# Sums and remainders on 32 columns of TensorE once per pair of rows, and the column sums of the last stage after the fill, in a fused backward kernel

## The chip, the cores and the metric

One core of a Trainium2 chip runs the whole program in one launch. The metric is the device time in microseconds (us) of that launch. The core has a matmul engine (TensorE, PE in the profile, its weight loads shown as PEld), three engines for elementwise work (VectorE, DVE; ScalarE, ACT; GpSimd, POOL) and SyncE (SP), which here only issues DMA transfers. ScalarE and GpSimd issue transfers too. Each engine works through its own list of instructions in order, and engines wait for each other through semaphores.

## The reference

The reference is one block of a network with 2048 rows and 576 columns in bfloat16: a modulation vector from `silu(c) @ w_mod`; LayerNorm, modulation, a spectral filter (`rfft2`, times `w_r + i w_i`, `irfft2`) and a residual; LayerNorm, modulation, a gated product and a residual. Its forward part is

```
mod = (silu(c) @ w_mod).reshape(1, 6, 1, 576)      # sa, ca, ga, sb, cb, gb
h = layernorm(x) * (1 + ca) + sa
x = x + ga * irfft2(rfft2(h) * (w_r + 1j * w_i))
h = layernorm(x) * (1 + cb) + sb
x = x + gb * (((h @ w_gate) * (h @ w_up)) @ w_down)
```

The kernel returns the output (o0) and the gradients with respect to x, w_r, w_i, w_gate, w_up, w_down, c and w_mod. For the modulation vectors it needs sums over all 2048 rows of products that the two LayerNorm backwards form; the change moves matmuls that make such sums.

## The kernel before

The 2048 rows are held as 16 "rows" of 128 partitions by 576 columns (row j below is such a slab, not a matrix row). SBUF is one tile, `arena`, cut by hand into views and rings, and PSUM is one tile, `bank`, of eight banks, so nearly all names in the profile are `arena` and `bank`, and instructions are told apart by their line. The order of TensorE's instructions is the order in which the program writes them. The other engines' orders, and those of their DMA queues, are set by a planner from costs and due times, so moving matmuls on TensorE can move instructions on every other engine.

The stages, in order: gradient of the gated product's output, and the forward spectral filter; forward and backward of the gated product in 18 blocks (lines 796 to 990, some 900 us); LayerNorm 2 backward; backward of the spectral filter (lines 1324 to 1361); the last stage, which is its last transform and LayerNorm 1 backward; a short end for the gradients of c and w_mod.

A `Fill` (line 163) is a list of closures with costs. `fill.run(us)` emits as many as its credit covers. In LayerNorm 2 backward the fill holds the weight gradients of the last two blocks: `gwd_halves` (line 882 on PE, its products read out by VectorE in 889 and 890), `gw_block` (904 and 908, read out by ScalarE in 909) and `gw_rem` (924, on 64 columns, read out in 930). From the backward of the spectral filter on, it holds the forward's last product, o0, in pieces of nine matmuls (`y_piece`, line 1106; four pieces make one half of a row, which ScalarE copies out in 1109; two banks take turns; VectorE finishes a row in 1112 and 1113, and 1115 stores it).

LayerNorm 2 backward is the loop `for j in range(19)` (line 1180). TensorE ends the last block's product (`gh2_last`, 963 to 966, added up by VectorE in 985) three rows and more ahead; the n of a row is loaded by SP (1064) into the space that this frees. For even j, `front` (1130 to 1136) and `back` (1142 to 1150) do the elementwise work of a pair of rows on VectorE and ScalarE. SP also issues the saved rows y (1068), the stores of gx (1147), tables (1173), and the transposes of the weight gradients (850). Then, on TensorE:

- `sums_1(j)`: two `quarter_sums`, four matmuls (line 1047) of 32 columns each, one in each column quarter of the array, that add row j to sums over all rows in bank 2. It ran once per row, at j + 1.
- `sums_2(i)`: the same form, four matmuls into bank 5, once per pair.
- `row_a(j)`: four full-width matmuls (line 443) that begin the next transform of row j and, for odd j, the four remainders of the pair (446 and 447, 32 columns each), read out by ScalarE in 453 and 461. Banks come from a ring of six that the fill uses too.

The sums are read at the end of this stage by VectorE (1257 and 1258). W rows for the next stage are loaded on SP (515, 517) and by GpSimd as indirect loads (518); GpSimd also clears and sets a small table `sel` (1250 to 1255).

The last stage is the loop `for j in range(18)` (line 1395). `stage_bi(j)` makes four full-width matmuls (579, 581) and two on 32 rows of the array (582, 583); ScalarE copies one bank (585), VectorE combines it with the other (587, 588). `column_sums` (line 1041: four matmuls on 64 columns, into banks 6 and 7) added row j - 2 to its sums. `stage_ai(j - 1)` (593, two full-width matmuls) gives gh, copied by ScalarE (1409). The row's elementwise work follows: 1411, 1418, 1419 and 1421 on ScalarE, 1415 to 1423 on VectorE, the store 1425 on GpSimd. Then 36 matmuls of fill per row. VectorE has further work between: `mod_grad` (1278, 1279), on w_mod loaded by SP (1274), stored by GpSimd (1282). x and gx rows are loaded by SP in 1072 into rings of four: x of row j + 2 is asked for at row j, and its buffer is that of row j - 2, last read by 1421. The rings gh and q, which `column_sums` reads, have three buffers. Other loads of this stage on SP are 1087 (operands of the fill) and 1099 (x1). At the end the sums are copied (1439) to R2, which feeds the gradients of c and w_mod (1443 to 1477) and the last part of out_8 (1457, 1459, 1462).

Of the kernel before, what the change touches and what calls it, by code (L numbers as in the profile page):

```python
# [81 lines left out]
def build(ctx, tc, A_x, A_w_r, A_w_i, B_w_gate, B_w_up, B_w_down, c_in, w_mod, grad_out,  # L82
          out_0, out_1, out_2, out_3, out_4, out_5, out_6, out_7, out_8):
    nc = tc.nc
    pe, ve, ac, po, sp = nc.tensor, nc.vector, nc.scalar, nc.gpsimd, nc.sync
# [124 lines left out]
    with tc.manual_schedule(engines={PE}):  # L210
# [115 lines left out]
        def single():  # L326
            sbank[0] = (sbank[0] + 1) % 3
            return sbank[0]
# [112 lines left out]
        def stage_a(fj, b):  # L441
            for m in range(4):
                mm(bank[:, b, 128 * m:128 * m + 128], fj[:, FB[m]:FB[m] + 128], bdf, True, True)

        def stage_a_rem(fj, b, sub):
            mm(bank[0:32, b, 128 * sub:128 * sub + 128], fj[:, 256:288], bdf, True, True)
            mm(bank[32:64, b, 128 * sub:128 * sub + 128], fj[:, 544:576], bdf, True, True)

        def evac_a(eng, b, j):
            dst = At[:, 0:4, :, 8 * j:8 * j + 8]  # L450
            src = bank[:, b, :].rearrange("p (m c b) -> p m c b", m=4, c=16)
            if eng is ac:
                ac.copy(dst, src)
            else:
                ve.tensor_copy(dst, src)

        def evac_rem(eng, brem, j0, n):
            dst = At[0:64, 4, :, 8 * j0:8 * (j0 + n)].rearrange("p c (j b) -> p j c b", j=n)
            src = bank[0:64, brem, 0:128 * n].rearrange("p (j c b) -> p j c b", j=n, c=16)
            if eng is ac:  # L460
                ac.copy(dst, src)
            else:
                ve.tensor_copy(dst, src)
# [155 lines left out]
        for jg in range(4):  # L619
# [8 lines left out]
            for jj in range(4):  # L628
                b = single()
# [156 lines left out]
        def sbk():  # L786
            sbank[0] += 1
            return sring[sbank[0] % len(sring)]
# [167 lines left out]
        def acc_b(j):  # L956

            return acc[:, j, 0:288].bitcast(BF)
# [20 lines left out]
        def gh2_last(j):  # L979

            for h in range(2):
                b = sbk()
                gh2_mms(NP - 1, j, h, bank[:, b, 0:288])
                hs = slice(288 * h, 288 * h + 288)
                tt(acc_b(j)[:, hs], acc[:, j, hs], bank[:, b, 0:288], ADD)
# [51 lines left out]
        def column_sums(srcs, b, j, w):  # L1037

            for h in range(2):
                for i, a in enumerate(srcs):  # L1040
                    mm(bank[w * i:w * i + w, b + h, 0:288], ones[:, 0:w], a[:, 288 * h:288 * h + 288], j == 0, j == 15, skip_group_check=True)

        def quarter_sums(a, b, q, start, stop):

            for h in range(2):
                r = slice(32 * (q + h), 32 * (q + h) + 32)
                mm(bank[r, b, 0:288], ones[:, 0:32], a[:, 288 * h:288 * h + 288], start, stop, skip_group_check=True)
# [14 lines left out]
        def load_n(j):  # L1062
            if j < 14:
                sp.dma_start(acc_h(j), n_d[:, j, :])

        def load_yl(i):
            yl[i] = yl_r.next()
            sp.dma_start(yl[i][:], y_d[:, 2 * i:2 * i + 2, :])
# [53 lines left out]
        st_a = {}  # L1122
# [4 lines left out]
        def front(i):  # L1127
            gn, t2, q, s = gn_r.next(), t2_r.next(), q_r.next(), s_r.next().rearrange("p (k v) -> p k v", k=2)
            n, opc = n_pair(i), two(mod[:, SCB, :])
            tt(gn[:], b_pair(i), opc, MUL)  # L1130
            tt(q[:], b_pair(i), n, MUL)
            tt(t2[:], q[:], opc, MUL)
            for k in range(2):
                j = 2 * i + k
                act(gn[:, k, :], gn[:, k, :], ACT.Copy, scale=rstd2[:, j:j + 1], accum_out=s[:, k, 0:1])
                act(t2[:, k, :], t2[:, k, :], ACT.Copy, scale=nrs2[:, j:j + 1], accum_out=s[:, k, 1:2])
            st_a[i] = (gn, t2, q, s)
# [14 lines left out]
        def sums_1(j):  # L1152
            quarter_sums(acc_b(j), 2, 0, j == 0, j == 15)
            quarter_sums(st_a[j // 2][2][:, j % 2, :], 2, 2, j == 0, j == 15)
# [3 lines left out]
                quarter_sums(st_a[i][1][:, k, :], 5, 2 * k, i == 0, i == 7)  # L1158

        def row_a(j):  # L1160
            Fj = st_a[j // 2][0]
            b = sbk()
            stage_a(Fj[:, j % 2, :], b)
            evac_a(ac, b, j)
            if j % 2:
                b = sbk()
                for i in range(2):
                    stage_a_rem(Fj[:, i, :], b, i)
                evac_rem(ac, b, j - 1, 2)

        def load_third(t, name, k):
            n = 1536
# [7 lines left out]
        for j in range(19):  # L1180
            want = min(16, 3 + 5 * j // 4)
            while done < want:
                gh2_last(done)
                done += 1
                if done < want:
                    fill.run(1.0)
            while loaded < min(done, j + 6):
                load_n(loaded)
                loaded += 1
            if j % 2 == 0 and j < 16:  # L1190
                front(j // 2)
                back(j // 2)
                if 2 <= j < 14:
                    load_yl(j // 2 + 1)
            if fill.left() > 12.0 or j > 15:
                fill.run(1.0 if j < 16 else 2.0)
            if 1 <= j < 17:
                sums_1(j - 1)
            if fill.left() > 12.0 or j > 15:
                fill.run(1.0)  # L1200
            if 3 <= j:
                if j % 2 == 0:
                    sums_2(j // 2 - 2)
                row_a(j - 3)
            if j == 4:
                sp.dma_start(TB.rearrange("p a b -> p (a b)"), tabs["TB"][:, :])
            if 6 <= j < 9:
                load_third(TC, "TC", j - 6)
            if j == 12:
                for i0 in range(9, 28, 5):  # L1210
                    load_wdr(i0, min(28, i0 + 5))
                for k in range(3):
                    load_third(TI, "TI", k)
                sp.dma_start(TBI.rearrange("p a b -> p (a b)"), tabs["TBI"][:, :])
            if j == 15:
                for t in W_r.t:
                    po.memset(t[:, :, :, DF:FP], 0.0)
                for u in range(2):
                    Ws[u] = W_r.next()
                    load_W(Ws[u], u)  # L1220
            if j == 16:
                load_wdr(0, 6)
# [171 lines left out]
        mdone, gq = 0, {}  # L1394
        for j in range(18):
            if j < 16:
                if j and j + 2 < 16:
                    load_xg(j + 2)
                Hs[j] = stage_bi(j, Gt, e_r, H_r)
            if j > 1:  # L1400

                column_sums(gq.pop(j - 2), 6, j - 2, 64)
            if j < 2:
                store_rev(6 + j, gws[6 + j])
            if 1 <= j < 17:
                jj = j - 1
                stage_ai(Hs[jj])
                gh = gh_r.next()
                ac.copy(halves(gh), bank[:, 2:4, 0:288])
                n = xl[jj]  # L1410
                act(n[:], n[:], ACT.Identity, bias=nmr1[:, jj:jj + 1], scale=rstd1[:, jj:jj + 1])
                gn, t2, q, s = tg_r.next(), t2_r.next(), q_r.next(), s_r.next()
                gq[jj] = [gh, q]
                opc = mod[:, SCA, :]
                tt(gn[:], gh[:], opc, MUL)
                tt(q[:], gh[:], n[:], MUL)
                tt(t2[:], q[:], opc, MUL)
                act(gn[:], gn[:], ACT.Copy, scale=rstd1[:, jj:jj + 1], accum_out=s[:, 0:1])
                act(t2[:], t2[:], ACT.Copy, scale=nrs1[:, jj:jj + 1], accum_out=s[:, 1:2])
                ts(s[:, 0:1], s[:, 0:1], -1.0 / D, None, MUL)  # L1420
                act(t2[:], n[:], ACT.Identity, bias=s[:, 0:1], scale=s[:, 1:2])
                tt(gn[:], gn[:], t2[:], ADD)
                tt(gn[:], gn[:], gl[jj][:], ADD)
                o1 = gn
                po.dma_start(o1_v[:, jj, :], o1[:])
                fill.run(2.2)
            fill.run(2.2)
            while mdone < min(18, 6 * j // 5):
                k, i = mdone // 3, mdone % 3
                mod_grad(*mgs[k], i)  # L1430
                if i == 2 and k + 2 < 6:
                    load_wm2(mgs[k + 2][0], mgs[k + 2][2])
                mdone += 1
            if 5 <= j < 14:
                i = j - 5
                sp.dma_start_transpose(out=wmT[:, i, :], in_=w_mod[:, 128 * i:128 * i + 128])
# [100 lines left out]
```

## Time and profile before

| | us |
|---|---|
| runs shown (five) | 1488.18 to 1492.09, median 1489.47 |
| profiled execution | 1490.96 |
| its span, first to last instruction | 1489.2 |
| PE busy in the span | 1449.6 (97%) |
| VectorE, ScalarE, GpSimd busy | 766.5, 540.7, 347.3 |
| mean granted TensorE clock | 0.994 |
| LayerNorm 2 backward, first to last sum (line 1047) | 1187.6 to 1262.8 |
| last stage, first to last column sum (line 1041) | 1378.2 to 1476.3 |

Times within the profile are us from the first instruction. Matmuls are pipelined: one of 288 columns is shown 0.29 us long, but a stream of them has a start every 0.12 us, so a busy PE says only that something was in it. What one costs is read from the distance of starts. "<-" names what ended an engine's wait. The granted clock is the share of full speed that TensorE had. A line number can be that of a helper that many places call.

### The profile page before, as it was taken

To read this page: it belongs to the slowest core of one execution; us is meant where nothing else is said; L and a number is where in the kernel's file an instruction comes from. 1 tells how busy PE (TensorE), PEld (TensorE's weight loads), DVE (VectorE), ACT (ScalarE), POOL (GpSimd) and SP (SyncE) were. 2 spreads that over 40 slices of the span, in tenths; PEclk is the share of its full clock that TensorE was granted. 3 is DMA by queue.
4 is the path that set the end of the run, shared out by engine and by line. 5 is a ranking of instruction groups with operands and counts; after the bars stand their busy time and mean duration, and the time that the engine had idled before them with its cause. 6 is when DMAs were issued, how large, how long until landed. Compare 5 with 4: busy or idle time off the path is not lost.

```text
span 1489.2 us, 28224 instructions
## 1 busy us (share of the span) xinstructions
PE 1449.6 (97%) x11085; PEld 975.9 (66%) x11108; DVE 766.5 (51%) x1651; ACT 540.7 (36%) x1048; POOL 347.3 (23%) x510
## 2 busy tenths in 40 slices
PE   8999998999999999999999999999999998999988
PEld 5444444677677677677677677677677666677666
DVE  6533596533543543543543543543443687677655
ACT  6756675212222222222222222222212366334565
POOL 1344322213213203203203203203202013332211
PEclk9999999999999999999999999999999999999999
DMA  9656886968568559559549558558548289667863
GB/s 340 185 150 158 230 238 163 206 147 190 119 120 192 122 115 195 126 108 198 127 105 194 122 112 202 116 111 202 130 93 184 75 245 309 215 187 206 260 201 96
DMA packets 417050, 252.79 MB, mean 170 GB/s; under 512 B 319730, under 2 KB 384692, under 8 KB 416660
## 3 DMA queue, kind: packets, MB, share of 16 engines
q1 hardware_dynamic: 388706, 166.53, 49.4%
q0 software_dynamic: 27440, 83.65, 18.6%
q8 instruction: 87, 1.43, 0.4%
q10 hardware_dynamic: 770, 0.80, 0.2%
q14 instruction: 47, 0.39, 0.1%
HBM read 98.52 MB, written 76.26 MB: 117 GB/s over the span
## 4 chain that ended last, share of the span: by engine, by line
PE 81%; DVE 7%; DMA 5%; ACT 4%; issue 2%; SPq 0%; DVEq 0%; ACTq 0%
PE bank L808 8%; PE bank L857 8%; PE bank L810 8%; PE bank L904 8%; PE bank L908 8%; PE bank L1106 6%; PE bank L963 5%; PE bank L965 5%; PE bank L966 5%; PE bank L964 5%; PE bank L371 3%; PE bank L375 3%; PE bank L802 2%; PE bank L924 2%; DMA arena<-in_w_mod_dram 2%
## 5 line engine op out<-in xcount | busy, mean ns | idle before, releaser
L977 DVE TENSOR_TENSOR arena<-arena,bank 128x576 f32<-128x576 f32 x256 | 193.1, 754 | 305.1 <-PE bank L966 305.1
L816 ACT CAST arena<-bank 128x512 bf16<-128x512 f32 x144 | 86.6, 602 | 396.2 <-PE bank L803 387.7
L966 PE MATMUL bank<-arena 128*128 128x288 bf16 x576 | 164.5, 286 | 0.0
L963 PE MATMUL bank<-arena 128*128 128x288 bf16 x576 | 164.0, 285 | 0.4 <-DVE arena L975 0.2
L965 PE MATMUL bank<-arena 128*128 128x288 bf16 x576 | 164.3, 285 | 0.0
L964 PE MATMUL bank<-arena 128*128 128x288 bf16 x576 | 164.1, 285 | 0.0
L1106 PE MATMUL bank<-arena 128*128 128x288 bf16 x1152 | 152.4, 291 | 4.5 <-ACT arena L1109 4.5
L904 PE MATMUL bank<-arena 128*128 128x256 bf16 x1152 | 149.5, 273 | 1.8 <-DVE arena L890 1.8
L908 PE MATMUL bank<-arena 128*128 128x256 bf16 x1152 | 149.3, 273 | 0.0
L808 PE MATMUL bank<-arena 128*128 128x512 bf16 x576 | 148.2, 380 | 0.0
L810 PE MATMUL bank<-arena 128*128 128x512 bf16 x576 | 147.8, 379 | 0.0
L1106 PEld LDWEIGHTS <-arena 128*128 128x128 bf16 x1152 | 113.5, 100 | 38.1 <-issue 7.3
L857 PE MATMUL bank<-arena 128*128 128x288 bf16 x1024 | 128.1, 286 | 0.0
L820 DVE TENSOR_TENSOR arena<-arena 128x512 bf16<-128x512 bf16 x144 | 60.8, 422 | 123.4 <-ACT arena L816 116.3
L904 PEld LDWEIGHTS <-arena 128*128 128x128 bf16 x1152 | 110.8, 98 | 18.6 <-issue 5.2
L908 PEld LDWEIGHTS <-arena 128*128 128x128 bf16 x1152 | 112.3, 98 | 13.7
L857 PEld LDWEIGHTS <-arena 128*128 128x128 bf16 x1024 | 100.2, 98 | 28.2
L735 POOL DMA_DIRECT2D arena<-ghh_d x36 | 19.9, 553 | 392.9 <-DVE arena L819 385.1
L909 ACT CAST arena<-bank 128x256 bf16<-128x256 f32 x144 | 52.6, 372 | 141.8 <-PE bank L908 141.6
L810 PEld LDWEIGHTS <-arena 128*128 128x128 bf16 x576 | 56.4, 98 | 68.0
L808 PEld LDWEIGHTS <-arena 128*128 128x128 bf16 x576 | 53.4, 98 | 71.7 <-issue 15.5
L817 ACT CAST arena<-bank 128x512 bf16<-128x512 f32 x144 | 85.7, 595 | 12.2 <-PE bank L810 11.6
(269 smaller groups left out, 2303.4 us busy)
## 6 DMA issues: line engine op xcount, KB each, us to landing
ghh_d<-arena POOLq DMA_DIRECT2D x72, 256.0 KB, 3.6
arena<-ghh_d POOLq DMA_DIRECT2D x36, 512.0 KB, 6.2
hh_d<-arena SPq DMA_DIRECT2D x36, 512.0 KB
arena<-hh_d SPq DMA_DIRECT2D x32, 576.0 KB
out_dram<-arena POOLq DMA_DIRECT2D x67, 144.0 KB, 4.3
out_dram<-arena POOLq DMA_DIRECT2D x36, 256.0 KB, 5.5
arena<-in_B_w_down_dram POOLq DMA_DIRECT2D x18, 288.0 KB, 4.8
arena<-in_B_w_gate_dram POOLq DMA_DIRECT2D x18, 256.0 KB, 3.5
```

The costliest lines, as they stand in the source:

```text
L808: mm(bank[:, bg, :], w[:, m, fs], h2T[:, js, m, :], k < 2 and m == 0, k > 1 and m == 3)
L810: mm(bank[:, bu, :], w[:, 4 + n, fs], h2T[:, js, m, :], k < 2 and n == 0, k > 1 and n == 3)
L816: ac.copy(g[:], bank[:, bg, :])
L857: mm(bank[:, b0 + h, 0:288], sf[:, 0, fb, j, :], go[:, j, 288 * h:288 * h + 288], j == 0, j == 15)
L904: mm(bank[:, st["b"], 0:256], h2p[:, j, 128 * m:128 * m + 128], sf[:, 1 + w, :, j, :], j == 0, False)
L908: mm(bank[:, st["b"], 0:256], h2p[:, j, 128 * m:128 * m + 128], sf[:, 1 + w, :, j, :], False, j == 15)
L963: mm(o, xT[:, 1, 0, cs], wT[p][:, 0, 0, hs], True, False)
L964: mm(o, xT[:, 2, 0, cs], wT[p][:, 0, 1, hs], False, False)
L965: mm(o, xT[:, 1, 1, cs], wT[p][:, 1, 0, hs], False, False)
L966: mm(o, xT[:, 2, 1, cs], wT[p][:, 1, 1, hs], False, True)
L977: tt(dst, dst, src, ADD)
L1106: mm(bank[:, yb, 0:288], hl[:, fb % 18, 128 * (j % 2):128 * (j % 2) + 128], wdr[:, fb, 288 * h:288 * h + 288], fb == 0, fb == 35)
```

## The change

In the loop of LayerNorm 2 backward, `row_a` is cut in two. `row_a(j)` keeps the four full-width matmuls; `rem_a(i)` has the four remainders of pair i. For even j the loop now emits, behind the fill and `row_a(j - 3)`, one run of 32-column matmuls: `rem_a` and `sums_2` of the pair two back, and `sums_1` of both rows of the last pair. For odd j it emits none. In the last stage `column_sums` of row j - 2 moves from between `stage_bi` and `stage_ai` to behind the fill. No matmul is added or taken away. All lines behind line 1160 shift by one to four.

```diff
@@ -1158,15 +1158,15 @@
                 quarter_sums(st_a[i][1][:, k, :], 5, 2 * k, i == 0, i == 7)
 
         def row_a(j):
-            Fj = st_a[j // 2][0]
             b = sbk()
-            stage_a(Fj[:, j % 2, :], b)
+            stage_a(st_a[j // 2][0][:, j % 2, :], b)
             evac_a(ac, b, j)
-            if j % 2:
-                b = sbk()
-                for i in range(2):
-                    stage_a_rem(Fj[:, i, :], b, i)
-                evac_rem(ac, b, j - 1, 2)
+
+        def rem_a(i):
+            b = sbk()
+            for k in range(2):
+                stage_a_rem(st_a[i][0][:, k, :], b, k)
+            evac_rem(ac, b, 2 * i, 2)
 
         def load_third(t, name, k):
             n = 1536
@@ -1194,14 +1194,18 @@
                     load_yl(j // 2 + 1)
             if fill.left() > 12.0 or j > 15:
                 fill.run(1.0 if j < 16 else 2.0)
-            if 1 <= j < 17:
-                sums_1(j - 1)
             if fill.left() > 12.0 or j > 15:
                 fill.run(1.0)
             if 3 <= j:
-                if j % 2 == 0:
-                    sums_2(j // 2 - 2)
-                row_a(j - 3)
+                row_a(j - 3)
+            if j % 2 == 0 and j >= 2:
+
+                if j >= 4:
+                    rem_a(j // 2 - 2)
+                    sums_2(j // 2 - 2)
+                if j < 18:
+                    sums_1(j - 2)
+                    sums_1(j - 1)
             if j == 4:
                 sp.dma_start(TB.rearrange("p a b -> p (a b)"), tabs["TB"][:, :])
             if 6 <= j < 9:
@@ -1397,9 +1401,6 @@
                 if j and j + 2 < 16:
                     load_xg(j + 2)
                 Hs[j] = stage_bi(j, Gt, e_r, H_r)
-            if j > 1:
-
-                column_sums(gq.pop(j - 2), 6, j - 2, 64)
             if j < 2:
                 store_rev(6 + j, gws[6 + j])
             if 1 <= j < 17:
@@ -1425,6 +1426,8 @@
                 po.dma_start(o1_v[:, jj, :], o1[:])
                 fill.run(2.2)
             fill.run(2.2)
+            if j > 1:
+                column_sums(gq.pop(j - 2), 6, j - 2, 64)
             while mdone < min(18, 6 * j // 5):
                 k, i = mdone // 3, mdone % 3
                 mod_grad(*mgs[k], i)
```

## The prediction

> **What bounds the kernel now.** First the page's busy shares, then the stages that the edit touches, then who waits there, then single instructions in order of time.
>
> The busy shares, then stretches of the two stages (us, then busy us of PE, PEld, DVE, ACT, POOL, then granted clock, DMA share, GB/s):
>
> ```profile
> PE 1449.6 (97%) x11085; PEld 975.9 (66%) x11108; DVE 766.5 (51%) x1651; ACT 540.7 (36%) x1048; POOL 347.3 (23%) x510
> ```
>
> ```profile
> 1232.00:1241.00 9.00, 6.82 (x49) 4.10 (x49) 9.00 (x20) 4.73 (x10) 2.03 (x2) 0.81 1.02 250
> 1241.00:1264.00 23.00, 22.35 (x245) 16.75 (x242) 15.47 (x27) 14.66 (x35) 10.64 (x22) 1.00 0.98 347
> ...
> 1372.00:1424.00 52.00, 44.59 (x355) 31.60 (x353) 33.10 (x97) 30.26 (x63) 12.70 (x22) 0.99 0.78 243
> 1424.00:1432.00 8.00, 8.00 (x43) 4.98 (x43) 7.59 (x22) 5.75 (x12) 1.74 (x3) 0.63 0.33 95
> ```
>
> PE is nearly full over the span, but not in the two edited stages. LayerNorm 2 backward runs from about 1187 to 1265: to 1241 VectorE is the full engine (9.00 of 9.00) and PE idles, from 1241 PE is full (22.35 of 23). The last stage runs from 1372 to the end: PE idles 7.4 us up to 1424, then works at a reduced clock, then is full. Who PE waits for, LayerNorm 2 first, then the last stage:
>
> ```profile
> PE bank L446 <- DVE arena L890: 3.3, 1, 3.3
> PE bank L904 <- DVE arena L890: 1.8, 1, 1.8
> ...
> PE bank L1106 <- ACT arena L1109: 4.5, 2, 3.9
> PE bank L581 <- DVE arena L588: 2.8, 3, 1.6
> ```
>
> The price of a small group on PE, and the column sums now, in order of time (start, length of the run):
>
> ```profile
> 1204.78 1.04 PE L904 MATMUL bank<-arena 128*128 128x256 bf16 x8
> 1205.74 0.31 PE L1047 MATMUL bank<-arena 128*32 128x288 bf16 x4
> 1205.98 1.05 PE L908 MATMUL bank<-arena 128*128 128x256 bf16 x8
> 1206.87 1.04 PE L904 MATMUL bank<-arena 128*128 128x256 bf16 x8
> 1207.74 0.39 PE L443 MATMUL bank<-arena 128*128 128x128 bf16 x4
> ...
> 1466.60 4.57 PE L1106 MATMUL bank<-arena 128*128 128x288 bf16 x36
> 1471.11 0.44 PE L1041 MATMUL bank<-arena 128*64 128x288 bf16 x4
> 1471.47 0.42 PE L593 MATMUL bank<-arena 128*128 128x288 bf16 x2
> ```
>
> Eight L904 followed by a full-width line take 0.87 (1206.87 to 1207.74); with four L1047 between they take 1.20 (1204.78 to 1205.98). Of the 0.33, one streaming time of 288 columns is 0.12 (L1106: 36 in 4.41, the four column quarters together); 0.21 is left for two changes of the array's shape, 0.105 each. L1041 gives the same: 36 x 0.1225 ends at 1471.01, L1041 starts 0.10 later, and L593 starts 0.36 after it, of which 0.245 is streaming.
>
> And the largest stall, with what it hangs on:
>
> ```profile
> 1415.63 0.33 SPq L1072 DMA_DIRECT2D arena<-in_A_x_dram  x1
> ...
> 1421.19 0.87 ACT L1411 ACTIVATE arena<-arena 128x576 bf16<-128x576 bf16 x1 [4.76 <-DMA arena<-in_A_x_dram]
> ...
> 1423.90 6.36 PE L1106 MATMUL bank<-arena 128*128 128x288 bf16 x27 [3.94 <-ACT arena L1109]
> ```
>
> ScalarE normalizes x three rows ahead (L1411 of row r+3 runs in row r), into a ring of four; the load can only be issued when L1421 of row r-1 has read the buffer. In row 6 L1411 stands ahead of L1418, L1419 and L1109 in ScalarE's order, so the copy of a finished y product waits for the x load, and PE for the copy: 3.94 us, and then 27 matmuls take 6.36 where 3.47 is the usual (at 1386.42): the clock was 0.63 over the next 8 us. Together 6.8 us. This loop (load, L1411, L1421, next load) paces rows 1 to 7: L593 comes every 7.3 us there and every 5.85 after.
>
> **The change part by part.** *Changes of shape in LayerNorm 2.* From PE's order in both kernels: 24 single groups of L1047 and 8 of remainders (L446, L447) become 9 runs. Counting every place where neighbours differ in tile shape, 68 become 25. 43 x 0.105 = 4.5 us of PE's time. No run longer than four L1047 is in the trace: in a run each further four could cost 0.12 (streaming; the remainders do it, two of 128 columns every 0.06 at 1203.57) or at worst the whole 0.24 that a lone group occupies (23 x 0.12 = 2.8 us given back). I take 0.12, since the remainders are the nearest row.
>
> *What of it reaches the end.* Up to 1239.4 PE is ahead of VectorE: it waits 1.8, 1.2 (L446 on ScalarE's L909) and 3.3 us, and VectorE waits for PE nowhere but at its first add (0.3) and at the end. What PE saves there it waits longer. The sums that stood ahead of the 3.31 wait (L446 on L890, 1233.89) now come after it, 12 L1047 in 0.37 us, and PE has until 1239.43, its next wait for L890, to do them: covered. SP's transposes wait for PE (L850 on L966, 6.4 us), so some of it may come back through the loads behind them on SP; on the other side one n_d load now stands behind a y_d load on SP. I put both at 0, within plus or minus 1.5 (half of the 3.7 us that VectorE waits for n_d at 1225.44). From 1239.4 to 1265 PE sets the time: 24 changes become 8, 1.7 us; but at 1252.26 L443 waits 0.65 for ScalarE's L930, and what lies before that can be lost in this wait; behind it 10 become 4, 0.6 us. I take 1.2, between the two.
>
> *W loads and sel.* On POOL the indirect loads L518 move behind memsets of `sel` and a gate-product store. They end at 1252.3 and are used from 1274.3 (L527): 20 us of cover, cost 0.
>
> *Column sums in the last stage.* They leave the place between the 32-row matmuls L582/L583 and L593, where they shared a change, for one between two full-width runs: 50 changes become 64. 14 x 0.105 = 1.5 us, of which rows up to 7 lie in the shadow of the x loop: 0.8 counts. Nothing waits for the sums but R2 at the end; their rings (three buffers) allow the later place.
>
> *The orders that move with it.* In row 6 ScalarE now has L1109, L1418, L1419 ahead of L1411; in row 2 too. SP issues one hh load (0.58 MB) instead of two between the w_mod loads and x of row 8, and gx ahead of both w_mod loads. POOL issues the o0 store ahead of two out_8 stores, and VectorE puts L1279 behind L1113 and L1420. Followed through, in the old clock: L1279 is about 1.25 late (1398.8), the w_mod loads go at 1402.9 and 1403.5 (1401.6, 1402.95 before), and land after 4.7 at 1408.2. VectorE then has one L1278 before L587 instead of L1278, L1422, L1279, L1423, L1278: L588 ends at 1409.7 for 1410.9, and PE's L581 of that row is 1.2 us earlier. Row 8's x, issued at 1406.75, took 6.3; with half of the hh bytes ahead it lands between 1410.8 and 1413.1. L1421 of row 5 ends at 1413.4 to 1415.6, x of row 9 lands 5.5 later, L1421 of row 6 ends at 1420.7 to 1422.9 (before 1424.6), x of row 10 lands 2.4 (as at 1424.65) to 5.5 later. Row 7 has L1411, L1418, L1109 in this order, so its copy is done 1.9 after that: 1425.0 to 1430.3. PE, with no wait in row 7's fill, needs that copy at 1424.55: L593 of row 7 at 1417.25 (1418.45 less 1.2), 0.25 of its streaming, 4.41 of fill, 0.45 of sums with two changes, 0.84 of L579 to L583, 0.25 of L593, and the 1.1 of nine fill matmuls that still have a bank. It waits 0.5 to 5.7; I take 2.4, since DMA is less busy by then (share 0.33 after 1424). The same point was at 1432.63: gain 5.7. A wait near 4 us cools the clock again (2.9); I count half: 4.2.
>
> The Trainium skill's "TensorE: Matmul & The Clock Gate" (Part 1) speaks against a PE that runs ahead: an idle window of about 3.4 us halves the clock. The trace agrees that 3.31 us of waiting brought the clock to 0.81 over 1232 to 1241. By the page alone each such wait would cost 1.7 us more (estimate from its 3.4 us window at half rate); by the row it costs nothing there, as VectorE is the full engine until 1241.
>
> *The end.* Sums of row 15 now come after 18 fill matmuls (2.2 us) instead of before. R2 is copied at about 1479.0 to 1479.6, L1443 is due at 1480.0: no wait. The out_8 scaling moves 2.2 us later on VectorE, partly ahead of L1448; PE's next need, L1467 at 1482.9, is still met. The last o0 row now stands behind L1475 and L1476: about 0.3 us, between 0 and 0.6.
>
> Sum: -1.2 - 4.2 + 0.8 + 0.3 = -4.3 us. The profiled execution took 1490.96 (span 1489.2); so 1486.7 for one like it. It lies 1.5 above the median, 1489.47, so the median should be 1485.2.
>
> **Rivals.** *A, the wait moves on.* Row 10's x comes at its late bound, PE waits about 5 us in row 8 and the clock drops: row 6's 6.8 us are paid in row 8. Then -1.2 + 0.8 + 0.3 - 0.3 = about -0.4: 1489. For it: row 7 has the very order that row 6 had. Against: the load that followed took 2.4 us.
> *B, slower: the o0 store blocks POOL.* The out_8 stores stand behind it; its waits were 7.9 us at 1387.9 and 3.0 at 1413.4. w_mod and, behind it on SP, x of row 8 have 3.2 us to spare (1403.5 to 1406.75). With 7.9, x comes 4.7 late, the loop carries it on, and PE cools (2.9): +7.6 on my sum, 1492.8. It decides from a wait of about 6 us.
> *C, PE's time counts everywhere.* SP's waits for PE pass the savings on in LayerNorm 2: -4.5 instead of -1.2, and row 8 waits only 0.5 us (-7.6): 1489.47 - 4.5 - 7.6 + 1.1 = 1478.5.
>
> **How the numbers follow.** Forecast 0.50, A 0.21, B 0.19, C 0.10. Less than 0.2% (3 us) is about what a measurement of this kernel can't tell from no change. Faster 0.58: C and nearly all of the forecast; same 0.22: A and a little of the forecast; slower 0.20: B. The range runs from 1479.5 (most of C) to 1493 (about half of B); the forecast's own is 1481.5 to 1488.
>
> **What would show it.** Right: L1047 in runs of 8 and 12 with 0.12 per four and 25 changes of shape; PE's wait before L446 near 1234 longer, the loop's end 0.6 to 1.7 earlier; no 3.9 us wait in row 6, a shorter one in row 8; clock not under 0.8 near 1424; L1041 with 0.1 on both sides. Wrong: runs of L1047 at 0.24 per four; a second stretch of low clock in the last stage; L1411 waiting longer in rows 5 to 8; x or w_mod loads issued later than in the old clock.

## The result and the profile after

The changed kernel takes 1486.34 us (median of 25 runs, 1483.01 to 1491.25); the kernel before took 1489.95 on the same chip (45 runs). The ratio is 0.9977, 95% interval 0.9971 to 0.9983: 3.4 us faster (2.5 to 4.3). The forecast was 4.3 us. Its execution with a profile took 1486.14 us, its span 1484.4.

First the page's busy shares after the change, then four of the stretches shown of before (us, busy us of PE, PEld, DVE, ACT, POOL, granted clock, DMA share, GB/s):

```profile
PE 1441.6 (97%) x11085; PEld 973.7 (66%) x11108; DVE 764.3 (51%) x1651; ACT 540.6 (36%) x1048; POOL 347.9 (23%) x510
```

```profile
1232.00:1241.00 9.00, 7.36 (x85) 5.53 (x85) 8.67 (x16) 4.16 (x10) 3.14 (x3) 1.00 1.02 295
1241.00:1264.00 23.00, 21.20 (x239) 17.27 (x238) 14.79 (x27) 15.09 (x36) 10.47 (x23) 1.00 0.97 346
1372.00:1424.00 52.00, 45.67 (x362) 31.50 (x360) 34.47 (x100) 31.56 (x65) 10.74 (x19) 0.99 0.76 243
1424.00:1432.00 8.00, 8.00 (x55) 5.26 (x54) 5.60 (x18) 6.04 (x14) 2.37 (x4) 0.82 0.58 176
```

The clock over 1232 to 1241 is 1.00 (0.81 before) and over 1424 to 1432 it is 0.82 (0.63 before). In the last stage PE still idles 6.3 us up to 1424. Who it waits for, LayerNorm 2 backward first, then the last stage:

```profile
PE bank L446 <- ACT arena L909: 2.6, 1, 2.6
PE bank L904 <- DVE arena L890: 1.9, 1, 1.9
PE bank L446 <- DVE arena L890: 1.7, 1, 1.7
PE bank L443 <- ACT arena L930: 1.7, 1, 1.7
PE bank L443 <- DVE arena L890: 1.6, 1, 1.6
...
PE bank L581 <- DVE arena L588: 4.6, 5, 1.5
PE bank L1106 <- ACT arena L1109: 2.3, 1, 2.3
```

In LayerNorm 2 PE waits more than before, in more places; in the last stage the 3.9 us for L1109 are gone, and there are more waits for L588. Now the two kinds of small groups, in order of time:

```profile
1202.94 0.23 PE L446 MATMUL bank<-arena 128*32 128x128 bf16 x1
...
1203.06 0.54 PE L1047 MATMUL bank<-arena 128*32 128x288 bf16 x10
1203.53 0.30 PE L963 MATMUL bank<-arena 128*128 128x288 bf16 x1
...
1420.41 0.44 PE L1041 MATMUL bank<-arena 128*64 128x288 bf16 x4
1420.78 0.42 PE L579 MATMUL bank<-arena 128*128 128x288 bf16 x2
1422.74 0.40 PE L581 MATMUL bank<-arena 128*128 128x288 bf16 x2 [1.54 <-DVE arena L588]
...
1423.30 0.53 PE L593 MATMUL bank<-arena 128*128 128x288 bf16 x2
1423.62 6.18 PE L1106 MATMUL bank<-arena 128*128 128x288 bf16 x36
```

Four remainders and twelve L1047 take 0.59 us (1202.94 to 1203.53), the change of shape at their end included; one pair of changes serves them all. Row 8 of the last stage shows what took the place of the old stall: a wait of 1.54 us for L588, and after it 36 matmuls in 6.18 us, where 4.57 is usual.

One profile is one draw. The executions of the kernel before spread over 7.6 us, and its stages vary as well; LayerNorm 2, counted from VectorE's first L1130 to TensorE's first L469, shows how far. The L443 at which PE waits for L890 near 1238 divides it in two. These lines are of the changed kernel:

```profile
1182.81 0.76 DVE L1130 TENSOR_TENSOR arena<-arena 128x1152 bf16<-128x1152 bf16 x1
```

```profile
1237.35 0.38 PE L443 MATMUL bank<-arena 128*128 128x128 bf16 x4 [1.64 <-DVE arena L890]
...
1262.89 0.41 PE L469 MATMUL bank<-arena 128*128 128x290 bf16 x2
```

That is 80.1 us, 54.5 up to this L443 and 25.5 behind it. Counted so in every profile of this study, with what the stage lost to the clock (one less the granted clock, times the length):

| LayerNorm 2 | profiles | us | up to L443 | behind L443 | lost to the clock |
|---|---|---|---|---|---|
| as before | 3 | 82.7, 83.1, 82.8 | 56.7 to 57.2 | 25.9 to 26.1 | 1.7 in each |
| as changed | 9 | 79.9 to 82.3, mean 81.0 | 54.3 to 56.7, mean 55.5 | 25.5 to 25.6 | 0 in two (79.9, 80.1), 1.7 in five (80.3 to 81.8), 3.4 in two (81.8, 82.3) |
| matmuls changed, other engines as before | 1 | 82.7 | 59.0 | 23.7 | 5.1 |
| matmuls as before, other engines as changed | 1 | 81.5 | 55.4 | 26.1 | 1.7 |

So the change is worth about 1.8 us here, not the 2.6 that the first two profiles alone would give: the changed kernel's first profile lost nothing to the clock in this stage. Among the profiles that lost 1.7 the difference is 1.8 as well (mean 81.1 against 82.8). All that was lost lies ahead of the L443, so the part behind it compares profiles at full clock.

### The profile page after: what moved, and what is told of

Its sections match the earlier page's. It is cut to its first block, busy times and chain, and to the rows that moved or that the text cites. A ratio compares the mean times of both kernels' runs of the same rounds, so it can differ in the third digit from the quotient of the medians.

```text
span 1484.4 us, 28222 instructions
## 1 busy us (share of the span) xinstructions
PE 1441.6 (97%) x11085; PEld 973.7 (66%) x11108; DVE 764.3 (51%) x1651; ACT 540.6 (36%) x1048; POOL 347.9 (23%) x510
## 3 DMA queue, kind: packets, MB, share of 16 engines
q8 instruction: 87, 1.43, 0.4%
## 5 line engine op out<-in xcount | busy, mean ns | idle before, releaser
L1106 PE MATMUL bank<-arena 128*128 128x288 bf16 x1152 | 149.8, 288 | 2.3 <-ACT arena L1109 2.3
L1106 PEld LDWEIGHTS <-arena 128*128 128x128 bf16 x1152 | 112.1, 98 | 34.5 <-issue 5.7
L909 ACT CAST arena<-bank 128x256 bf16<-128x256 f32 x144 | 52.5, 372 | 137.5 <-PE bank L908 137.1
L817 ACT CAST arena<-bank 128x512 bf16<-128x512 f32 x144 | 85.7, 595 | 12.2 <-PE bank L810 11.6
```

The costliest lines, as they stand in the source:

```text
L1106: mm(bank[:, yb, 0:288], hl[:, fb % 18, 128 * (j % 2):128 * (j % 2) + 128], wdr[:, fb, 288 * h:288 * h + 288], fb == 0, fb == 35)
```

## The experiments

Unless said otherwise, lines are numbered as in the changed kernel: L1412 is L1411 of before, L1282 is L1278, L1410 is L1409, L1422 is L1421. Rows of the last stage are counted by their L593, from 0; the stall of before at 1423.90, which the prediction calls row 6's after ScalarE's work, lies behind the L593 of row 7. Gains are worked out as the ratio's distance from 1 times the median of before in the same comparison (1488.2 to 1489.2).

### The two halves, each alone

The half in LayerNorm 2 (first part of the diff) and the half in the last stage (the moved `column_sums`), each on the kernel before. Outside the edited stage the orders of the four other engines come out as before, inside it as in the changed kernel.

> Only the half of the change in LayerNorm 2 backward; the column sums of the last stage stay where they were. The other engines' orders are those of the changed kernel in LayerNorm 2 and those of the kernel before in the last stage. Theory 'halves add' (the changed kernel's first L593 came 3.6 us earlier, its end another 1.2 earlier): the lead of 3.6 us at the first L593 survives the last stage, 3 to 3.6 us faster than before, with a wait of PE for L1109 near 4 us in row 6. Rival 'the loop of the x loads swallows the lead' (it paces rows 1 to 7 whatever PE does): less than 1 us faster, and the wait in row 6 longer by what was gained ahead of it.

> Only the half of the change in the last stage: column sums behind the fill, LayerNorm 2 backward as before. The other engines' orders are those of the kernel before up to the last stage and those of the changed kernel in it. Theory 'halves add': the loop of LayerNorm 2 ends as before, no wait of 3.9 us in row 6, and 1 to 1.6 us faster than before. Rival 'the forecast's last stage': all that the forecast gave to the last stage is found here, 3 to 4 us faster. Rows 8 and up have a period of 5.95 us by both (5.85 before).

LayerNorm 2 alone: 0.9987 (0.9979 to 0.9996), 1.9 us faster. The last stage alone: 0.9994 (0.9983 to 1.0005), 0.9 faster, which can't be told from nothing. Together 2.8, near the 3.4 of both. The first lies between the 3 to 3.6 us of its theory and the less than 1 of its rival, and its interval touches both. The second is compatible with the 1 to 1.6 of its theory and not with the 3 to 4 of its rival, which is what the forecast gave to the last stage. The stall that the forecast priced has neither a fixed place nor a fixed size. With the last stage ordered as before, the first run's profile has (all of the last stage, us, times, longest):

```profile
PE bank L1106 <- ACT arena L1109: 5.5, 3, 2.3
```

They are in rows 3, 7 and 10 (2.27, 1.84, 1.43), so 1.84 us where the profile of before has 3.94, and the clock drops at the one in row 3 alone; from the first L593 to the end of the span the stage took 113.6 us, against 116.5 in the profile of before. The second run, with the changed order, also took 113.6.

### Matmuls against the other engines' orders

The change moves matmuls; a planner then reorders all other engines. Two kernels take these apart. Both add a function that ties the instructions of VectorE, ScalarE, GpSimd and SyncE, from LayerNorm 2 on, in a given order. `mine` is the list of that engine's instructions as written, `ranks` the order wanted. The ties order issue on one engine and add no wait.

```diff
+    for name, (first, ranks) in ORDERS.items():
...
+        for a, b in zip(ranks, ranks[1:]):
+            tc.add_manual_dep(mine[b], mine[a].name, info, reason="order")
```

> All matmuls in the order of the changed kernel, but the instructions of VectorE, ScalarE, GpSimd and SyncE held in the order that they had before. Theory 'the gain is reordering': no gain, within 1 us of before or slower (VectorE's wait of 3.7 us for n_d near 1225 and the long wait in row 6 are back; fewer changes of shape give about 1.2 us in LayerNorm 2, and 14 more of them in the last stage take 0.8 to 1.5). Rival 'the gain is PE's time': 2 us faster or more.

> All matmuls in the order that they had before, but the instructions of VectorE, ScalarE, GpSimd and SyncE held in the order of the changed kernel. Theory 'the gain is reordering': 3 us faster than before or more (VectorE's chain about 2 us earlier at 1232, no wait near 4 us in row 6, and 14 changes of shape fewer in the last stage than the changed kernel has). Rival 'the gain is PE's time': within 1 us of before.

Changed matmuls with the old orders: 1.0016 (1.0004 to 1.0027), 2.4 us slower. Old matmuls with the new orders: 0.9978 (0.9967 to 0.9989), 3.3 us faster, as much as the whole change. The gain is the reordering: the two intervals lie on opposite sides of 1. With the new orders the moved matmuls, 43 changes of shape fewer in LayerNorm 2 and 14 more in the last stage taken together, are worth about nothing within these intervals; with the old ones they cost.

What they cost there shows in the clock. This is the first kernel (old orders), PE's waits in LayerNorm 2, then three stretches of it:

```profile
PE bank L904 <- DVE arena L890: 2.2, 1, 2.2
PE bank L446 <- ACT arena L909: 2.1, 1, 2.1
PE bank L446 <- DVE arena L890: 2.1, 1, 2.1
PE bank L904 <- DVE arena L985: 1.9, 1, 1.9
```

```profile
1200.00:1212.00 12.00, 10.09 (x104) 8.25 (x102) 8.13 (x17) 6.66 (x17) 0.00 (x0) 1.00 0.59 195
1212.00:1220.00 8.00, 5.92 (x47) 4.12 (x46) 7.14 (x15) 6.19 (x15) 0.78 (x1) 0.57 1.14 229
1232.00:1240.00 8.00, 5.93 (x49) 4.04 (x48) 7.21 (x16) 4.73 (x10) 0.00 (x0) 0.79 1.07 218
```

The whole stage, in the kernel before and in this one:

```profile
1182.65:1265.31 82.66, 75.17 (x731) 55.23 (x729) 68.01 (x130) 53.05 (x121) 19.23 (x31) 0.98 0.87 262
```

```profile
1182.34:1265.04 82.70, 73.01 (x731) 57.50 (x729) 67.55 (x130) 53.28 (x121) 20.10 (x31) 0.94 0.87 247
```

A PE that needs less time for its sums gets to the same gates sooner and stands there longer: 9.5 us of waits in LayerNorm 2 against 7.4 before, two of them (1.89 and 2.08, at 1210.86 and 1214.19) with little between, and the clock at 0.57 and 0.79. The mean granted clock over 12 executions was 0.9931, against 0.9956 over 35 of before: 10.3 us lost to the clock instead of 6.5 (one less the clock, times the mean span). These 3.8 us are more than the whole loss, and executions with the same clock take about the same time: at 0.994, four of this kernel took 1488.23 to 1490.45 us and eight of before 1487.99 to 1492.11. The second kernel has 0.9965, 5.2 us. That the longer waits are what lowers the clock is read from this profile and not shown beyond it: the changed kernel's profile has 10.8 us of waits in this stage at a clock of 1.00. Two other costs of this kernel are not taken apart either: VectorE waits 2.2 us for the moved sums (L1131 on L1047, twice; not at all in the profile of before), and the last stage has its 14 further changes of shape.

What the new orders do in LayerNorm 2 is seen on VectorE. In the prediction's profile L1131 waited 3.71 us for n_d at 1225.44, with L1130, which was ready, behind it:

```profile
1225.44 0.76 DVE L1131 TENSOR_TENSOR arena<-arena 128x1152 bf16<-128x1152 bf16 x1 [3.71 <-DMA arena<-n_d]
...
1226.97 0.75 DVE L1130 TENSOR_TENSOR arena<-arena 128x1152 bf16<-128x1152 bf16 x1
```

The same place in the changed kernel:

```profile
1222.78 0.76 DVE L1130 TENSOR_TENSOR arena<-arena 128x1152 bf16<-128x1152 bf16 x1 [0.88 <-PE bank L447]
1224.85 0.76 DVE L1131 TENSOR_TENSOR arena<-arena 128x1152 bf16<-128x1152 bf16 x1 [1.31 <-DMA arena<-n_d]
```

L1130 now stands ahead; n_d comes about as late, but less of VectorE's time is lost, and PE's L446 gets its bank from L890 at 1232.00 instead of 1233.89. This is no draw of one profile: counted from VectorE's first L1130, that L446 comes after 49.0 to 51.4 us in the ten profiles with the new orders (49.7 with the matmuls as before) and after 51.2 to 52.5 in the four with the old ones (means 49.8 and 51.6).

Behind the L443 of the table PE's own saving can be seen. With the old orders it is there: 23.7 us instead of 25.9, about the 1.7 of the forecast's 16 changes of shape and the 0.65 of a wait for L930 that is gone. From that kernel:

```profile
1241.30 0.38 PE L443 MATMUL bank<-arena 128*128 128x128 bf16 x4 [1.05 <-DVE arena L890]
...
1265.04 0.41 PE L469 MATMUL bank<-arena 128*128 128x290 bf16 x2
```

With the new orders 0.3 us of it are left: in each of the nine profiles PE waits 1.7 us at a later L443 for ScalarE's L930, where it waited 0.65 before.

### The price of a change of shape

Two kernels that keep all other engines' orders as in the changed kernel and move only column sums: back to their old place, and cut in two halves around the last 18 fill matmuls.

```diff
+            if j > 1:
+                column_sums(gq[j - 2], 6, j - 2, 64, (0,))
             fill.run(2.2)
             if j > 1:
-                column_sums(gq.pop(j - 2), 6, j - 2, 64)
+                column_sums(gq.pop(j - 2), 6, j - 2, 64, (1,))
```

> The changed kernel with the column sums back between the 32-row matmuls and L593, all other engines' orders held as in the changed kernel. Theory '0.1 us per change of shape where PE sets the pace': rows from 9 on have a period of 5.85 instead of 5.95, and the total is 0.5 to 1.5 us below the changed kernel's, 4 to 5 below before. Rival 'the position of the sums costs nothing': 3.4 below before, as the changed kernel.

> The changed kernel with each row's column sums in two halves (two matmuls ahead of the last 18 fill matmuls, two behind them), all other orders held: two more changes of shape per row and no more matmuls. Theory '0.105 us per change': period of rows from 9 on 6.16 instead of 5.95. Rival 'only the first group of a kind costs': 5.95 to 6.0.

The halves, over one row in which PE waits for nothing:

```profile
1437.03 0.42 PE L593 MATMUL bank<-arena 128*128 128x288 bf16 x2
1437.29 2.37 PE L1106 MATMUL bank<-arena 128*128 128x288 bf16 x18
1439.59 0.31 PE L1041 MATMUL bank<-arena 128*64 128x288 bf16 x2
1439.83 2.38 PE L1106 MATMUL bank<-arena 128*128 128x288 bf16 x18
1442.14 0.31 PE L1041 MATMUL bank<-arena 128*64 128x288 bf16 x2
...
1443.21 0.42 PE L593 MATMUL bank<-arena 128*128 128x288 bf16 x2
```

Rows follow each other at 6.18 us, against 5.95 in the changed kernel and 5.85 with the sums in their old place: 0.11 to 0.12 for each of the two added changes, 0.10 for the one saved. The price of the forecast, 0.105, holds. In the total, the sums in their old place gave 0.9972 (0.9958 to 0.9985), 4.2 us faster than before: on the expected side of the changed kernel, but not separable from it. The halves had one run, 1487.62, which says nothing about a total.

### Five buffers instead of four for x and gx

The changed kernel, and the half in LayerNorm 2, each with a fifth buffer.

```diff
-        x_r = Ring(span(RA, 3, 1152) + [ACC + 14464], [D])
-        gl_r = Ring(span(RA + 3456, 3, 1152) + [ACC + 15616], [D])
+        x_r = Ring(span(RA, 3, 1152) + [ACC + 14464, ACC + 16768], [D])
+        gl_r = Ring(span(RA + 3456, 3, 1152) + [ACC + 15616, ACC + 17920], [D])
```

> The changed kernel with five buffers instead of four in the rings of x and gx rows, so that a load waits for L1422 of a row one further back. Theory 'the loop of x loads paces rows 1 to 7': PE's waits for L588 (4.6 us together) and for L1109 (2.3) go, rows follow each other every 5.95 us from the first on, and the nine rows that took 61.9 us take 53.6: about 8 us faster than the changed kernel, 11 to 12 faster than before. Rival 'the transfers are late by themselves' (DMA busy 0.78 there): less than 2 us faster than the changed kernel.

> Five buffers as in the run before, with the half of the change in LayerNorm 2 alone: column sums between the 32-row matmuls and L593, as before the change. If the loop of x loads is gone, PE sets the pace of the last stage, and the 14 changes of shape that the moved sums add count in every row: period 5.85 instead of 5.95, 1 to 1.5 us faster than the run before, 12 to 13 faster than before. Rival 'a change of shape is hidden': same time as the run before within 0.5.

0.9963 (0.9950 to 0.9977) and 0.9957 (0.9941 to 0.9974): 5.5 and 6.4 us faster than before, 2 and 3 more than the changed kernel, where 8 more and over were expected. The theory of the loop was half right. ScalarE in the first of the two:

```profile
1414.63 0.87 ACT L1412 ACTIVATE arena<-arena 128x576 bf16<-128x576 bf16 x1 [3.41 <-DMA arena<-in_A_x_dram]
1415.41 0.38 ACT L585 COPY arena<-bank 128x288 f32<-128x288 f32 x1
```

It still waits for x, 13.3 us together in these rows, 5 times (11.6 in the changed kernel): the planner uses the fifth buffer to put L1412 still further ahead, here ahead of a copy (L585) that PE's L579 needs. This points at the place of L1412 and not at the ring.

### L1412 held in its own row

`tc.keep_in_program_order` holds an instruction behind all that was written before it for its engine. First L1412 alone: on the changed kernel, on its half in LayerNorm 2, and on the kernel before.

```diff
-                act(n[:], n[:], ACT.Identity, bias=nmr1[:, jj:jj + 1], scale=rstd1[:, jj:jj + 1])
+                tc.keep_in_program_order(act(n[:], n[:], ACT.Identity, bias=nmr1[:, jj:jj + 1], scale=rstd1[:, jj:jj + 1]))
```

> The changed kernel, with L1412 (n of a row from x, on ScalarE) held right behind L1410 of its own row, instead of one to three rows ahead. Theory 'ScalarE's early L1412 is what blocks': x has then been asked for two rows, about 12 us, before it is used; PE's waits for L1109 (2.3 us) and L588 (4.6 us) in rows 1 to 8 shrink to under 2 us together, rows follow each other at 5.95 to 6.2 us, and the kernel is 5 to 8 us faster than the changed one, 8 to 11 faster than before. Rival 'DMA is too slow for these rows': L1412 waits in its own row, and no more than 2 us are gained on the changed kernel.

> As the run before, with the column sums between the 32-row matmuls and L593, as before the change. With PE setting the pace, 14 changes of shape fewer: period 5.85 us, 1 to 1.5 us faster than the run before. Rival (a change of shape hides beside other waits): within 0.5 of it.

> The kernel before, with L1411 held right behind L1409 of its own row. If the reordering of ScalarE is all that the moved column sums brought, the wait of 3.9 us in row 6 goes here too, and this kernel beats the changed one: 6 to 9 us faster than before, and 1 to 2 slower than the run before this, which has in addition the half of the change in LayerNorm 2. Rival 'the sums' place matters by itself': the wait in row 6 stays at 2 us or more.

0.9980 (0.9970 to 0.9991), 3.0 us faster than before; 0.9954 (0.9938 to 0.9971), 6.8; 0.9982 (0.9972 to 0.9991), 2.7. In their profiles ScalarE waits for x no more, and PE no more for L1109, in any of the three. But the changed kernel gains nothing by it (3.4 without), and what was expected came in none: 8 to 11 us, 1 to 1.5 more than that, and 6 to 9. The wait moved. VectorE in the first of the three, 1369 to 1430 (us, times, longest):

```profile
DVE arena L1282 <- DMA arena<-in_w_mod_dram: 10.8, 3, 5.6
```

L1282, the product with w_mod, stands up to six rows ahead of its place as well. The second kernel shows the chain, VectorE and then PE:

```profile
1402.97 0.76 DVE L1282 SCALAR_TENSOR_TENSOR arena<-arena 128x576 bf16<-128x576 bf16 x1 [3.52 <-DMA arena<-in_w_mod_dram]
...
1405.71 0.45 DVE L588 TENSOR_TENSOR arena<-arena,bank 128x288 bf16<-128x288 f32 x1
```

```profile
1406.21 0.41 PE L581 MATMUL bank<-arena 128*128 128x288 bf16 x2 [2.02 <-DVE arena L588]
```

In the changed kernel the same wait, 1.66 us at 1421.19, stands ahead of the L588 for which PE waited 1.54 us in row 8. The first and the second kernel differ in the place of the column sums alone in what is written, yet by 3.8 us: about 1.4 of it is fourteen changes of shape at 0.10; the rest is seen only as longer waits in the first one's profile (2.17 and 3.12 us for L588, the clock at 0.60 and 0.68 behind them) and was not taken further apart.

### L1282 held in its place too

The half in LayerNorm 2, L1412 held, and L1282 as well.

```diff
-            ve.scalar_tensor_tensor(out=pr_t[:], in0=w[:, i, :], scalar=1.0, in1=rows, op0=MUL, op1=MUL, accum_out=gsc[:, m, s0 // 2 - 1:s0 // 2])
+            tc.keep_in_program_order(ve.scalar_tensor_tensor(out=pr_t[:], in0=w[:, i, :], scalar=1.0, in1=rows, op0=MUL, op1=MUL, accum_out=gsc[:, m, s0 // 2 - 1:s0 // 2]))
```

> As the run with the half of the change in LayerNorm 2 and n held in its own row; in addition the product with w_mod on VectorE (L1282) is held at its place in the program, instead of up to six rows ahead. There it waited 4.6, 3.5 and 2.1 us for its w_mod load, with L587 and L588 of the next row behind it. Theory 'an early instruction that waits for a transfer blocks what is queued behind it': PE's waits for L588 (4.6 us there) go, rows follow each other at 5.85 us from the first on, 5 to 7 us faster than that run, 11 to 13 faster than before. Rival 'the transfers of these rows are late wherever they are used': waits of VectorE or ScalarE for x, w_mod or gx of 2 us or more remain in rows 1 to 8, and less than 2 us are gained.

1477.31 us (1476.13 to 1477.83, 6 runs), 0.9917 (0.9903 to 0.9932): 12.4 us faster than before, 9 faster than the changed kernel. The two stretches of the last stage in it:

```profile
1372.00:1424.00 52.00, 52.00 (x429) 37.88 (x428) 39.55 (x108) 40.87 (x82) 12.33 (x21) 1.00 0.75 235
1424.00:1432.00 8.00, 8.00 (x68) 5.97 (x67) 7.67 (x22) 6.40 (x12) 2.37 (x5) 1.00 1.03 379
```

PE is busy 52.00 of 52.00 us at full clock (45.67 in the changed kernel), and waits for nobody until the end of the loop; rows follow each other every 5.85 us from the first. The DMA share is 0.75 (0.76 in the changed kernel), so the transfers were not too slow; they were waited for too early. The total is what the theory expected, and its rival's waits are gone: VectorE and ScalarE wait for no transfer in these rows. L1282 held alone was not tried. The executions lie within 1.7 us of each other, where those of before spread over 7.3 in the same comparison.

## Why the prediction was right or wrong

**Changes of shape, 0.105 us each, and 0.12 per further four L1047.** Right on both: 0.10 and 0.11 in the runs above, and 12 L1047 with four remainders in 0.59 us. The longer runs cost only their streaming.

**What of it reaches the end of LayerNorm 2, 1.2 us.** The size was near: the half alone gave 1.9 us (0.6 to 3.1), the profiles 1.8. The cause was not the forecast's. It took the 1.2 from PE's own time behind 1239.4 and put VectorE's chain at 0 within 1.5 us. Behind that point the changed kernel gained 0.3, not 1.2: the saving is there when the old orders are held (2.1 us), but with the new ones PE's wait for L930 grew from 0.65 to 1.7 and took it. The forecast had seen this wait and not that it would grow. The other 1.4 lie ahead of that point, and the one profile with the new orders alone has them too (55.4 us instead of 56.9). So two steps failed: the 1.2, and the 0 for the chain, where L1130 went ahead of the wait for n_d, and L890 came 1.9 us earlier in the first profile. The forecast followed the other engines' new orders through the last stage, step by step, and not through this one.

**"PE's wait before L446 near 1234 longer".** Wrong in the profile after (1.74 us instead of 3.31), because VectorE was early. That PE runs ahead and waits longer is what the kernel with the old orders shows.

**The clock, by row and by rule.** The forecast set a row, where 3.31 us of waiting and a clock of 0.81 cost nothing since VectorE was full, against a rule that every such wait costs 1.7 us. With the old orders the rule was the better guide: 3.8 us more were lost to the clock and 2.4 us in total, though other costs may have a part in that. With the new orders no such loss is seen (0.9965 with the old matmuls, 0.9959 over 27 executions of the changed kernel).

**The last stage, 4.2 us less 0.8 and 0.3.** Mis-sized. The half alone gave 0.9 us (from 0.7 lost to 2.5 gained). The stall did go, and a shorter wait with one cooling came in row 8, as written: 1.54 us and 1.6 of clock, for 2.4 and half of 2.9. But it came by another way, VectorE's L1282 waiting for w_mod and not ScalarE's L1411 for x; and a wait that was not foreseen came in row 2, 2.35 us, behind an L1412 that stood 5.03 us for x. The deeper error is the 6.8 us that were set against it. That was the largest stall of one execution; in another one with the same orders it was 1.84 us, with two more waits elsewhere, and the stage was 2.9 us shorter.

**Fourteen more changes and the end, 0.8 and 0.3.** Rows from 9 on have 5.95 instead of 5.85; the stretch from L1446 (L1443 before) to the end of the span is 9.6 us against 9.2. Both held.

**The rivals.** A, the wait that moves on to row 8, is half of what was seen. B, the o0 store in front of the out_8 stores, was seen in part: GpSimd waited 2.97 us ahead of that store, until 1397.69, and the out_8 stores behind it went at 1398.24, as late as before (1398.22) although the stage had begun 3.6 us earlier. The x load that was at stake went at 1405.08 (1406.75 before), 2.0 us later counted from the first L593, a sign of being wrong by the forecast's own list. How much of that is B is open, since the wait in row 2 had delayed the rows by then; it stayed short of the 6 us from which B was to decide. C, that PE's time counts everywhere, fell with the two kernels with exchanged orders.

That the sum was near is in part luck: two errors, 0.7 us too little in LayerNorm 2 and about 2 too much in the last stage, partly cancelled.

## What to carry to other kernels

Where a planner sets the order of the other engines, an edit on one engine is first an edit of all the others' orders: hold these orders fixed in one kernel, and the engine's own order in another, before giving the gain to the edit. An instruction that depends on a transfer and is put early on an in-order engine makes all behind it wait for the transfer; a deeper ring may only let it be put earlier still, and holding two such instructions at their place was worth 12.4 us here with the LayerNorm 2 half, where the planned change was worth 3.4. A stall seen in one execution is a draw: price it from several, or from what makes it possible.

## What the runs showed of the hardware

In the stages from LayerNorm 2 to the end of the last loop the granted clock is 1.00 or 0.50, in every profile, and it stays at 0.50 for 3.4 us or twice that; it was so over 1235.3 to 1238.7 in the kernel before:

```profile
1235.27:1238.68 3.41, 3.41 (x18) 1.81 (x17) 3.41 (x8) 1.77 (x5) 0.11 (x1) 0.50 0.98 254
```

The 0.81 or 0.63 of a longer stretch is a mean of the two.

The same matmuls behind the same waits ran at different clocks in different executions. After waits of 0.79, 0.78 and 0.81 us within 4.4 us in the stage behind LayerNorm 2 there are 27 L1106. The kernel before, the changed kernel, and the fastest kernel:

```profile
1273.34 4.91 PE L1106 MATMUL bank<-arena 128*128 128x288 bf16 x27
```

```profile
1270.68 3.47 PE L1106 MATMUL bank<-arena 128*128 128x288 bf16 x27
```

```profile
1271.74 5.14 PE L1106 MATMUL bank<-arena 128*128 128x288 bf16 x27
```

Two of the fourteen profiles have the slow form. So a clock window of one profile is no property of the kernel. The Trainium skill's "TensorE: Matmul & The Clock Gate" (Part 1, What's actually happening) says that the gate looks through a free-running window of some 3.4 us, so that the moment of a change depends on where in the window the work falls. That agrees with one stretch having both clocks. It also says that the clock falls after a window of idling; here it fell behind those three short waits, and behind one of 1.54 us in row 8, with work between, so a window need not be idle throughout.
